# Pooled attention and mixture of depths: the gate taken from the router's scores instead of the gathered rows, and three gathers moved between two chunks' attention

## The chip, the cores and the metric

The kernel runs on one core of one Trainium2 chip. The metric is the device time of one execution in microseconds (us). The median of three runs before the change is 248.09 us (247.69 to 248.15). The profiled execution is a run of 246.4 us whose span, from its first to its last instruction, is 244.6 us. The engines are called as the profile calls them: PE multiplies matrices (PEld is its weight load), DVE and ACT are the vector and the scalar engine, POOL is GpSimd, SP only issues transfers.

## The reference

Two blocks follow each other: attention over keys and values that are averaged in groups of eight, and a feed-forward layer that only the 128 best-scored rows of each batch go through.

```python
B, H, S, D = q.shape                      # 8, 8, 576, 64
k_p = k.reshape(B, H, S//8, 8, D).mean(axis=3)
v_p = v.reshape(B, H, S//8, 8, D).mean(axis=3)
attn = softmax(q @ k_p^T / sqrt(D))       # 576 x 72 for each head
x = (attn @ v_p), heads side by side      # (8, 576, 512)

scores = x @ w_gate                       # (8, 576)
out = x.copy()
for b in range(B):
    top_idx = the 128 rows with the largest scores[b]
    h  = np.maximum(x[b, top_idx] @ w1, 0.0)     # 512 -> 1024
    ye = h @ w2                                  # 1024 -> 512
    g  = 1.0 / (1.0 + np.exp(-scores[b, top_idx]))
    out[b, top_idx] = x[b, top_idx] + g[:, None] * ye
```

The gate g of a chosen row is a function of its score alone, and the score has been computed once already, for all rows, to choose the 128.

## The kernel before, in words

**Attention.** The 576 rows of a batch are cut into chunks of 128 rows. The loop over u (21 units, 0 to 20) takes two chunks at a time: a batch has two units of two chunks each, and the 64 rows left over from two neighbouring batches share one chunk, which is a unit of its own. For an even batch e from 2 on, with s = 6, 11, 16 for e = 2, 4, 6, the units are s and s+1 (batch e), s+2 (the shared chunk of e and o = e+1) and s+3, s+4 (batch o). In each unit `attend` multiplies exponentials with values for both chunks on PE (L371, into the two buffers of the accumulator pA), `norm` divides by the softmax sums on DVE (L379, L387) and puts the scores of the rows into `scs` (L396), `scores` of the next unit runs on PE (L344), its exponentials on ACT (L355 and L349), and `store_x` writes the finished rows to the output (L416, issued by ACT).

**The scores.** The values carry one column more, the pooled value times w_gate (`share_v` L273 on POOL, `gate_v` L277 on DVE), so that attention itself gives the score of every row.

**Choosing and gathering.** `row_bcast` (L438, PE) spreads a batch's scores over all partitions, `count` (L450 and L454, DVE) counts for each row how many are larger, `one_hot` sums the counts on PE (L462) and makes a one-hot matrix OH on DVE (L463, L465). `gather` multiplies OH with `auxb` on PE (L475): auxb holds for each row its number in two bfloat16 parts, so that the two columns of the product add up to the number of the chosen row (`tok`, L477, DVE). POOL turns it into an index (L479) and issues an indirect transfer (L481) that reads the chosen rows back from the output in DRAM into `xr`. It can start only when the batch's stores have landed.

**The feed-forward layer.** `x_trans` transposes xr on PE (L512), `hidden` (L525) and `finish` (L538) are its two products, in float32. `gate` works out g: DVE multiplies xr (128x512) with w_gate, writes the product into `y` (which is only scratch for it) and keeps the sum of each row (L491); ACT takes the exponential (L493); `gate_end` adds one and inverts on DVE (L497, L498). `finish` computes y = p * g + xr on DVE (L539), and POOL scatters y into the output (L541).

**What sets the order.** Nothing is reordered by a scheduler: each engine executes its instructions in the order in which the program emits them. The order around the change is written by hand with `at(u, slot, job)`: a unit runs its attends, slot -1, the norms, slot 0, the next unit's scores, slot 0.5, the stores, and slots 1 to 4. PSUM tiles named `bank` rotate over four banks, which the scores of the next unit all need. POOL also pools keys and values (L246, L247 and L264 to L266); a value pooled late delays `gate_v`, and that the attention which reads the value's extra column.

Of the kernel before, what the change touches and what calls it, by code (L numbers as in the profile page):

```python
# [7 lines left out]
FT = mybir.dt.float32  # L8
BF = mybir.dt.bfloat16
I32 = mybir.dt.int32  # L10
AF = mybir.ActivationFunctionType
OP = mybir.AluOpType
AX = mybir.AxisListType
# [35 lines left out]
def direct_path(ctx, tc, q, k, v, moe_w_gate, moe_w1, moe_w2, moe_capacity, out, flag):  # L49
# [22 lines left out]
    nc = tc.nc  # L72
# [9 lines left out]
    NC = 5  # L82
    C = 128
    HG = H // 2
    R = 2 * TG // POOLW
    DM = H * D
# [4 lines left out]
    cap = int(moe_capacity)  # L91
# [5 lines left out]
    const = ctx.enter_context(tc.tile_pool(name="const", bufs=1))  # L97
# [85 lines left out]
    ones = const.tile([C, 1], BF)  # L183
    one32 = const.tile([C, 1], FT)
    rzall = const.tile([C, NCH, H], FT)
    auxb = [const.tile([C, NC, 2], BF, name=f"auxb{i}") for i in range(2)]
    w1 = const.tile([128, DB, F], FT)
    w2 = const.tile([128, FB, DM], FT)

# [42 lines left out]
    def bank(shape, i=None):  # L232

        if i is None:
            i = turn[0]
        turn[0] = (i + 1) % 4
        return psum.tile(shape, FT, name=f"bank{i}", bufs=1)
# [202 lines left out]

    def count(b):

        CN[b] = work.tile([C, NC], FT, name="cns")
        GE[b] = [work.tile([C, c + 1, C], BF, name=f"ge{c}", bufs=1) for c in range(NC)]
        k = cn[b % 2]
        for c in range(NC):
            s = scs[b % 2][:, c : c + 1]
            n = min(c + 1, NC - 1)
            if c == NC - 1:
                nc.vector.tensor_scalar(GE[b][c][:, 0:n, :], SR[b][0], s, None, op0=OP.is_ge, op1=OP.add,  # L450
                                        accum_out=k[:, c, 1:2])
            x, y, m = ((GE[b][c], SR[b][0][:, 0:n, :], before[:, NC - 1 - n :, :]) if c < NC - 1 else
                       (GE[b][c][:, c : c + 1, :], SR[b][1], before[:, NC - 2 : NC - 1, :]))
            nc.vector.scalar_tensor_tensor(x, y, s, m, op0=OP.is_ge, op1=OP.mult, accum_out=k[:, c, 0:1])  # L454
        nc.vector.tensor_reduce(out=CN[b], in_=k, axis=AX.X, op=OP.add)

    def one_hot(b):

# [11 lines left out]

    def gather(b):

        p = bank([cap, 2], 0 if b == 0 else None)
        for c in range(NC):
            nc.tensor.matmul(p, OH[b][:, c, :], auxb[b % 2][:, c, :], start=(c == 0), stop=(c == NC - 1))  # L475
        tok = work.tile([cap, 1], FT, name="tok")
        nc.vector.tensor_reduce(out=tok, in_=p, axis=AX.X, op=OP.add)  # L477
        idx = work.tile([cap, 1], I32, name="idx")
        nc.gpsimd.tensor_scalar(idx, tok, float(S - 1), float(b * S), op0=OP.min, op1=OP.add)  # L479
        XR[b] = work.tile([cap, DM], FT, name="xr", bufs=3)  # L480
        i = nc.gpsimd.indirect_dma_start(  # L481
            out=XR[b], out_offset=None, in_=out_rows[0 : (b + 1) * S], in_offset=bass.IndirectOffsetOnAxis(ap=idx[:, :1], axis=0))
        others(i, b, (store, scat))
        gath[b] = [i]
        GV[b] = (idx, work.tile([cap, 1], FT, name="g"))

    def gate(b):

        idx, g = GV[b]
        Y[b] = work.tile([cap, DM], FT, name="y")  # L490
        nc.vector.scalar_tensor_tensor(Y[b], XR[b], 1.0, wg[:cap].rearrange("p h d -> p (h d)"), op0=OP.mult, op1=OP.mult,  # L491
                                       accum_out=g)
        nc.scalar.activation(g, g, AF.Exp, scale=-1.0)  # L493

    def gate_end(b):
        idx, g = GV[b]
        nc.vector.tensor_scalar(g, g, 1.0, None, op0=OP.add)  # L497
        nc.vector.reciprocal(g, g)  # L498
# [30 lines left out]
    def finish(b, part, parts, p):  # L529

        idx, g = GV[b]
        if part == 0 and b > 1:
            gate_end(b)
        c = slice(DM // parts * part, DM // parts * (part + 1))
        p = p.rearrange("p a b -> p (a b)")[:cap, 0 : DM // parts]
        for f in range(FB):
            n, m = divmod(f, FB // 2)
            nc.tensor.matmul(p, HT[b, n][:, m, :], w2[:, f, c], start=(f == 0), stop=(f == FB - 1))  # L538
        nc.vector.scalar_tensor_tensor(Y[b][:, c], p, g, XR[b][:, c], op0=OP.mult, op1=OP.add)  # L539
        if part == parts - 1:  # L540
            i = nc.gpsimd.indirect_dma_start(  # L541
                out=out_rows, out_offset=bass.IndirectOffsetOnAxis(ap=idx[:, :1], axis=0), in_=Y[b], in_offset=None)
            others(i, b, (store, scat, gath))
            scat[b] = [i]
# [34 lines left out]
    def at(u, slot, *job):  # L579
        jobs.setdefault((u, slot), []).append(job)  # L580


    pool = nc.gpsimd
    at(2, 2, row_bcast, 0)
    at(2, 2, count, 0)
    at(3, -1, one_hot, 0)
    at(3, -1, gather, 0)
# [7 lines left out]
    at(4, 1, dense, hidden, 0, 0, True)  # L595
    at(4, 1, dense, hidden, 0, 1)
    at(4, 1, k_trans, 2)
    at(4, 1, gate, 0)
    at(4, 1, gate_end, 0)
    at(5, 0, gate_v, 2, 0)  # L600
    at(5, 0, gate_v, 2, 1)
    at(5, 1, row_bcast, 1)
    at(5, 1, count, 1)
    at(5, 1, dense, finish, 0, 0, True, 2)
    at(5, 2, one_hot, 1)
    at(6, -1, gather, 1)
    at(6, 1, dense, finish, 0, 1, True, 2)
    at(7, 0.5, x_trans, 1)
    at(7, 0.5, gate, 1)
    at(8, 1, gate_end, 1)  # L610
    at(7, 2, dense, hidden, 1, 0, True)
    at(8, 2, dense, hidden, 1, 1)
# [2 lines left out]
    for e in range(2, B, 2):  # L615
        s = 6 + 5 * (e // 2 - 1)
        o, last = e + 1, e + 2 == B
        for f in (row_bcast, count):
            at(s + 2, 1, f, e)
            at(s + 4, 0 if last else 1, f, o)  # L620
        at(s + 2, 3, one_hot, e)
        at(s + 3, 3, gather, e)
        if last:
            at(s + 4, 3, x_trans, e)
            at(s + 4, 4, gate, e)
            for f, *x in ((dense, hidden, e, 0), (one_hot, o), (dense, hidden, e, 1), (gather, o), (set_flag,),
                          (dense, finish, e, 0, False, 2), (x_trans, o), (dense, finish, e, 1, False, 2), (gate, o),
                          (dense, hidden, o, 0), (dense, hidden, o, 1), (dense, finish, o, 0)):
                at(s + 5, 1, f, *x)
        else:  # L630
            at(s + 4, 3, one_hot, o)
            at(s + 4, 4, x_trans, e)
            at(s + 4, 4, gate, e)
            at(s + 5, 3, gather, o)
            at(s + 6, 3, x_trans, o)
            at(s + 6, 3, gate, o)
            at(s + 5, 1, dense, hidden, e, 0, True)
            at(s + 5, 2, dense, hidden, e, 1)
            at(s + 6, 1, dense, finish, e, 0, True)
# [15 lines left out]
            at(s + 2, 1, load_v, y)  # L655
            at(s + 2, 2, load_q, y)
            at(s + 2, 4, pool_k, x, pool)
            at(s + 2, 4, pool_v, x, 0, pool, False)
            at(s + 3, 4, share_v, x, 0, pool)
            at(s + 3, 4, pool_v, x, 1, pool)  # L660
            at(s + 3, 0.5, k_trans, x)
            at(s + 4, 1, gate_v, x, 0)
# [25 lines left out]
    def run(u, slot):  # L688
        for f, *x in jobs.pop((u, slot), ()):
            f(*x)  # L690
# [23 lines left out]
    for u in range(NU + 1):  # L714
        mine = [a for a, x in enumerate(chunks) if x[0] == u]
        for a in mine:
            attend(a)
        run(u, -1)
        for a in mine:
            norm(a)  # L720
        run(u, 0)
        if u + 1 < NU:
            scores(u + 1)
        run(u, 0.5)
        if u < NU:
            store_x(u)
        if u + 2 < NU:
            q_trans(u + 2)
        for slot in range(1, 5):
            run(u, slot)  # L730
# [357 lines left out]
```

## Time and profile before

| | |
|---|---|
| device time, median of three | 248.09 us |
| span of the profiled execution | 244.6 us |
| PE busy | 224.1 us (92%) |
| DVE busy | 142.1 us (58%) |
| POOL busy | 130.6 us (53%) |
| ACT busy | 63.6 us (26%) |
| `y<-xr,wg` L491 on DVE | 8 times, 0.68 us median, 3.69 us the longest |
| `tok<-bank` L477 on DVE | 8 times, 0.16 us median |
| `xr<-out_dram,idx`, from issue to landing | 3.4 us the shortest, 4.2 median, 8.4 the longest |

PE is busy nearly all the time, and its idle time is the difference between 244.6 and 224.1 us: 20.5 us, of which 6.7 lie in the first 40 us and 7.6 in the last 15. In the view by windows a row gives the stretch, its length, and for each engine the busy time and the number of instructions; length less PE's busy time is PE's idle time there. In the timeline a row is a start time, a duration, engine, line, operation, and in brackets the time that the engine stood idle before it with what ended the wait. Times on the timeline are counted from the start of the span.

### The profile page before, as it was taken

The page shows a single profiled execution, that of the slowest core. Times are in us where ns is not written, and L with a number is a line of the kernel's source. Part 1 is how long each engine was busy: PE and PEld are TensorE (multiplying, and loading weights), DVE is VectorE, ACT ScalarE, POOL GpSimd, SP SyncE. Part 2 cuts the span into 40 slices and gives each one's busy share as a digit, 9 for nine tenths or more (in the row PEclk, how much of TensorE's full clock was granted, in tenths as well). Part 3 has the DMA queues.
Part 4 walks back from the last instruction along what each step waited for, and adds up shares of the span by engine and source line. Part 5 has one row for each costly group of instructions (what it writes and reads, how often), then busy time and mean ns, then how long its engine had stood idle before and what let it go on. Part 6 is the DMA issues. An engine that isn't in the chain of part 4 may idle for free.

```text
span 244.6 us, 7008 instructions
## 1 busy us (share of the span) xinstructions
PE 224.1 (92%) x2928; PEld 185.0 (76%) x2930; DVE 142.1 (58%) x423; ACT 63.6 (26%) x183; POOL 130.6 (53%) x127
## 2 busy tenths in 40 slices
PE   8989868999999999799989999979989999989980
PEld 4658647899879988699658994769568999979830
DVE  5989776738757878861538957782347337212010
ACT  8233403213311432231113323041114300111100
POOL 8659917995595559596929356594720020121001
PEclk9999999999999999999999999999999999999998
DMA  7999998699716999999509342120411131110001
GB/s 262 349 397 348 381 379 312 204 362 307 256 68 161 366 373 373 383 373 372 187 0 324 155 129 88 44 87 3 131 44 46 47 119 55 43 46 28 19 7 48
DMA packets 14400, 46.94 MB, mean 192 GB/s; under 512 B 1432, under 2 KB 3480, under 8 KB 12312
## 3 DMA queue, kind: packets, MB, share of 16 engines
q1 hardware_dynamic: 9880, 32.77, 37.8%
q10 hardware_dynamic: 3200, 9.44, 11.4%
q0 software_dynamic: 1280, 4.20, 5.2%
q8 instruction: 25, 0.41, 0.7%
q14 instruction: 15, 0.12, 0.2%
HBM read 34.87 MB, written 11.53 MB: 190 GB/s over the span
## 4 chain that ended last, share of the span: by engine, by line
PE 47%; DMA 23%; POOL 13%; DVE 6%; issue 6%; SPq 1%; POOLq 0%; ACT 0%; ACTq 0%
PE bank L538 10%; PE bank L525 9%; PE bank L344 7%; PE pA L371 7%; PE pA L525 6%; PE pA L538 6%; DMA qraw<-in_q_dram 5%; DMA vraw<-in_v_dram 5%; DMA xr<-out_dram,idx 5%; POOL vraw L264 4%; DMA w<-in_moe_w_dram 4%; DMA out_dram<-xs 3%; POOL vraw L265 2%; POOL vp L266 1%; DMA out_dram<-y,idx 1%
## 5 line engine op out<-in xcount | busy, mean ns | idle before, releaser
L355 ACT ACTIVATE et<-bank 128x256 f32<-128x256 f32 x128 | 37.1, 411 | 62.8 <-PE bank L344 62.8
L344 PE MATMUL bank<-qt,kt 32*128 32x256 f32 (+1 forms) x768 | 40.7, 349 | 0.3 <-DVE tok L477 0.3
L525 PE MATMUL bank<-xg,w 128*128 128x128 f32 x320 | 37.6, 276 | 0.2
L371 PE MATMUL pA<-vp,et 128*64 128x66 f32 x1024 | 34.5, 224 | 3.3 <-DVE vp L277 2.3
L525 PEld LDWEIGHTS bank<-xg,w 128*128 128x128 f32 x320 | 36.6, 192 | 1.0 <-ACT et L355 0.9
L371 PEld LDWEIGHTS pA<-vp,et 128*64 128x64 f32 x1024 | 32.1, 137 | 5.7 <-ACT et L355 2.9
L344 PEld LDWEIGHTS bank<-qt,kt 32*128 32x128 f32 x768 | 32.6, 185 | 2.9 <-DVE tok L477 0.3
L264 POOL TENSOR_TENSOR vraw<-vraw 128x1024 f32<-128x1024 f32 x14 | 33.1, 2362 | 2.8 <-DMA vraw<-in_v_dram 2.7
L541 POOL DMA_INDIRECT out_dram<-y,idx x8 | 9.0, 1120 | 45.5 <-DVE y L539 38.3
L538 PE MATMUL bank<-w,ht 128*128 128x256 f32 (+1 forms) x112 | 32.6, 444 | 0.2
L538 PEld LDWEIGHTS bank<-w,ht 128*128 128x128 f32 x112 | 20.7, 190 | 9.3 <-issue 6.7
L538 PE MATMUL pA<-w,ht 128*128 128x256 f32 (+1 forms) x80 | 25.3, 469 | 0.0
L525 PE MATMUL pA<-xg,w 128*128 128x128 f32 x192 | 23.3, 278 | 1.7 <-DVE rzall L379 1.6
L525 PEld LDWEIGHTS pA<-xg,w 128*128 128x128 f32 x192 | 22.0, 192 | 3.5 <-issue 3.0
L329 DVE STREAM_TRANSPOSE qt<-qraw 128x1024 f32<-128x1024 f32 (+1 forms) x24 | 23.0, 967 | 1.5 <-DMA qraw<-in_q_dram 1.5
L479 POOL TENSOR_SCALAR idx<-tok 128x1 int32<-128x1 f32 x8 | 1.8, 223 | 40.0 <-DVE tok L477 36.5
L387 DVE TENSOR_TENSOR xs<-pA,rzall 128x512 f32<-128x512 f32 x32 | 22.1, 691 | 1.1
L538 PEld LDWEIGHTS pA<-w,ht 128*128 128x128 f32 x80 | 14.8, 190 | 8.6 <-issue 7.0
L246 POOL TENSOR_TENSOR kraw<-kraw 128x1152 f32<-128x1152 f32 x7 | 18.5, 2637 | 4.8 <-DVE ge L454 4.7
L539 DVE SCALAR_TENSOR_TENSOR y<-bank,g,xr 128x256 f32<-128x256 f32 (+1 forms) x7 | 3.9, 559 | 26.4 <-PE bank L538 26.4
L265 POOL TENSOR_TENSOR vraw<-vraw 128x512 f32<-128x512 f32 x14 | 17.8, 1271 | 1.1
L454 DVE SCALAR_TENSOR_TENSOR ge<-pA,sc,before 128x128 bf16<-128x128 f32 (+3 forms) x35 | 16.2, 507 | 1.3 <-PE pA L438 1.2
(105 smaller groups left out, 241.6 us busy)
## 6 DMA issues: line engine op xcount, KB each, us to landing
kraw<-in_k_dram SPq DMA_DIRECT2D x8, 1152.0 KB, 9.6
qraw<-in_q_dram SPq DMA_DIRECT2D x8, 1152.0 KB, 13.5
out_dram<-xs ACTq DMA_DIRECT2D x32, 256.0 KB, 3.0
vraw<-in_v_dram SPq DMA_DIRECT2D x7, 1024.0 KB
w<-in_moe_w_dram SPq DMA_DIRECT2D x1, 2048.0 KB
w<-in_moe_w_dram SPq DMA_DIRECT2D x2, 1024.0 KB, 8.6
vraw<-in_v_dram SPq DMA_DIRECT2D x2, 512.0 KB, 7.0
out_dram<-xh ACTq DMA_DIRECT2D x8, 128.0 KB, 6.2
```

The costliest lines, as they stand in the source:

```text
L246: eng.tensor_tensor(out=x[:, :, 0:2, :], in0=x[:, :, 0:2, :], in1=x[:, :, 2:4, :], op=OP.add)
L264: eng.tensor_tensor(out=x[:, :, 0:4, :], in0=x[:, :, 0:4, :], in1=x[:, :, 4:8, :], op=OP.add)
L265: eng.tensor_tensor(out=x[:, :, 0:2, :], in0=x[:, :, 0:2, :], in1=x[:, :, 2:4, :], op=OP.add)
L329: nc.vector.transpose(out=QT[u][:, :, n : n + x.shape[1], :].rearrange("p j t c -> p t j c"), in_=x)
L344: nc.tensor.matmul(p[i][:, s, n, :], KT[x][r, j, s, :], QT[u][r, j, t, G * s : G * s + G], start=(j == 0), stop=(j == 1))
L355: nc.scalar.activation(ET[u][c][i].rearrange("p s (n g t) -> p (s n) g t", n=2, g=G), p[i].rearrange("p s one (n t c g) -> p (s one n) c g ...
L371: nc.tensor.matmul(PA[a][TL * t : TL * t + TL, g, E * n : E * n + E], e, VP[b][:, h, :], start=True, stop=True)
L387: nc.vector.tensor_tensor(out=y[r, i, :].rearrange("p (g n d) -> p g n d", g=2, d=D), in0=o[:, :, :, 0:D], in1=rz.rearrange("p g (n one) - ...
L454: nc.vector.scalar_tensor_tensor(x, y, s, m, op0=OP.is_ge, op1=OP.mult, accum_out=k[:, c, 0:1])
L525: nc.tensor.matmul(p[:, n, :], w1[:, d, 128 * f : 128 * f + 128], XG[b][:, d, :], start=(d == 0), stop=(d == DB - 1))
L538: nc.tensor.matmul(p, HT[b, n][:, m, :], w2[:, f, c], start=(f == 0), stop=(f == FB - 1))
L541: i = nc.gpsimd.indirect_dma_start(out=out_rows, out_offset=bass.IndirectOffsetOnAxis(ap=idx[:, :1], axis=0), in_=Y[b], in_offset=None)
```

## The change

The gate is no longer computed from the gathered rows. A new function `pieces` splits the float32 score of each row into three bfloat16 pieces on POOL: the rounded score, the rounded rest, and the rest of that. They lie beside the two parts of the row number in auxb, so the same five products of `gather` carry them along, with five columns instead of two. One more reduction on DVE adds the three columns of a chosen row to its score. The product of xr and w_gate on DVE goes away, and with it the need to have the gathered row before the gate. `y` is now allocated in `finish`.

Some jobs move. For the even batches 2, 4 and 6 the gather goes from the end of unit s+3 to a new slot -2, between the attends of that unit's two chunks. In the same units the pooling of the next even batch's first half of values is emitted behind the gather, in slot -1 (before: its adds at the end of unit s+2, ahead of the gather, and its product with w_gate behind the gather). The exponential of the gate is emitted soon after its gather. At the end of the program the one-hot and the gather of batch 7 each go ahead of one half of the hidden product of batch 6.

```diff
-    auxb = [const.tile([C, NC, 2], BF, name=f"auxb{i}") for i in range(2)]
+    auxb = [const.tile([C, NC, 5], BF, name=f"auxb{i}") for i in range(2)]
...
-        CN[b] = work.tile([C, NC], FT, name="cns")
+        CN[b] = work.tile([C, NC], FT, name="cns", bufs=1)
...
+    def pieces(b):
+        s, a = scs[b % 2], auxb[b % 2]
+        rest = work.tile([C, NC], FT, name="rest", bufs=1)
+        nc.gpsimd.tensor_copy(a[:, :, 2], s)
+        nc.gpsimd.tensor_tensor(out=rest, in0=s, in1=a[:, :, 2], op=OP.subtract)
+        nc.gpsimd.tensor_copy(a[:, :, 3], rest)
+        nc.gpsimd.tensor_tensor(out=a[:, :, 4], in0=rest, in1=a[:, :, 3], op=OP.subtract)
...
     def gather(b):
-        p = bank([cap, 2], 0 if b == 0 else None)
+        p = bank([cap, 5], 0 if b == 0 else None)
...
-        nc.vector.tensor_reduce(out=tok, in_=p, axis=AX.X, op=OP.add)
+        nc.vector.tensor_reduce(out=tok, in_=p[:, 0:2], axis=AX.X, op=OP.add)
...
-        GV[b] = (idx, work.tile([cap, 1], FT, name="g"))
+        g = work.tile([cap, 1], FT, name="g")
+        GV[b] = (idx, g)
+        nc.vector.tensor_reduce(out=g, in_=p[:, 2:5], axis=AX.X, op=OP.add)
     def gate(b):
         idx, g = GV[b]
-        Y[b] = work.tile([cap, DM], FT, name="y")
-        nc.vector.scalar_tensor_tensor(Y[b], XR[b], 1.0, wg[:cap].rearrange("p h d -> p (h d)"), op0=OP.mult, op1=OP.mult,
-                                       accum_out=g)
         nc.scalar.activation(g, g, AF.Exp, scale=-1.0)
...
     def finish(b, part, parts, p):
-        if part == 0 and b > 1:
-            gate_end(b)
+        if part == 0:
+            Y[b] = work.tile([cap, DM], FT, name="y")
+            if b > 1:
+                gate_end(b)
...
+    at(2, 2, pieces, 0)
...
-    at(4, 1, gate, 0)
+    at(3, 1, gate, 0)
...
+    at(5, 1, pieces, 1)
...
-    at(7, 0.5, gate, 1)
+    at(6, 1, gate, 1)
...
+        at(s + 2, 1, pieces, e)
+        at(s + 4, 0 if last else 1, pieces, o)
         at(s + 2, 3, one_hot, e)
-        at(s + 3, 3, gather, e)
+        at(s + 3, -2, gather, e)
+        at(s + 3, 3, gate, e)
         if last:
             at(s + 4, 3, x_trans, e)
-            at(s + 4, 4, gate, e)
-            for f, *x in ((dense, hidden, e, 0), (one_hot, o), (dense, hidden, e, 1), (gather, o), (set_flag,),
-                          (dense, finish, e, 0, False, 2), (x_trans, o), (dense, finish, e, 1, False, 2), (gate, o),
+            for f, *x in ((one_hot, o), (dense, hidden, e, 0), (gather, o), (dense, hidden, e, 1), (gate, o), (set_flag,),
+                          (dense, finish, e, 0, False, 2), (x_trans, o), (dense, finish, e, 1, False, 2),
                           (dense, hidden, o, 0), (dense, hidden, o, 1), (dense, finish, o, 0)):
...
-            at(s + 4, 4, gate, e)
             at(s + 5, 3, gather, o)
             at(s + 6, 3, x_trans, o)
-            at(s + 6, 3, gate, o)
+            at(s + 5, 4, gate, o)
...
-            at(s + 2, 4, pool_v, x, 0, pool, False)
-            at(s + 3, 4, share_v, x, 0, pool)
+            at(s + 3, -1, pool_v, x, 0, pool)
             at(s + 3, 4, pool_v, x, 1, pool)
...
         for a in mine:
             attend(a)
+            if a == mine[0]:
+                run(u, -2)
         run(u, -1)
```

## The prediction

> **What bounds the kernel now.** I read the page's busy times first, then the windows, then who waited for whom, and last the timeline around each wait of PE. PE is busy for 224.1 of 244.6 us, so the time is PE's work plus PE's idle time. The windows say where the idle time lies:
>
> ```profile
> 88.00:104.00 16.00, 14.66 (x203) 12.35 (x199) 12.21 (x35) 5.33 (x18) 12.19 (x11) 1.00 1.02 387
> 104.00:120.00 16.00, 16.00 (x273) 14.65 (x269) 8.35 (x26) 4.72 (x14) 13.77 (x11) 1.00 0.89 325
> 120.00:140.00 20.00, 19.34 (x240) 14.68 (x240) 12.04 (x38) 4.50 (x14) 11.46 (x9) 1.00 0.51 171
> 140.00:160.00 20.00, 19.31 (x261) 13.95 (x259) 13.70 (x34) 5.07 (x17) 11.22 (x10) 1.00 0.26 80
> 160.00:180.00 20.00, 19.00 (x221) 14.82 (x223) 8.49 (x27) 4.77 (x15) 12.53 (x11) 1.00 0.23 67
> 180.00:200.00 20.00, 19.34 (x319) 17.77 (x320) 11.84 (x45) 6.62 (x20) 2.52 (x3) 1.00 0.18 56
> 215.00:230.00 15.00, 14.01 (x98) 12.88 (x97) 1.95 (x7) 1.41 (x4) 2.27 (x2) 1.00 0.11 37
> ```
>
> Length less PE's busy time, the second and third numbers, is 1.34, 0, 0.66, 0.69, 1.00, 0.66 and 0.99 us: 5.3 us of idle time between 88 and 230 us, in small pieces. The clock (1.00) is full everywhere. The DMA share next to last says that transfers fill the engines until about 120 us and have room afterwards. PE's waits in the timeline are these:
>
> ```profile
> 102.49 0.63 PE L512 MATMUL bank<-ident,xr 128*128 128x128 f32 x4 [1.25 <-DMA xr<-out_dram,idx]
> ...
> 127.34 0.68 PE L371 MATMUL pA<-vp,el 128*64 128x66 f32 x14 [0.62 <-DVE vp L277]
> ...
> 161.00 2.25 PE L525 MATMUL pA<-xg,w 128*128 128x128 f32 x18 [1.59 <-DVE rzall L379]
> ...
> 181.30 0.68 PE L371 MATMUL pA<-vp,el 128*64 128x66 f32 x14 [0.62 <-DVE vp L277]
> ...
> 219.26 0.63 PE L512 MATMUL bank<-ident,xr 128*128 128x128 f32 x4 [0.99 <-DMA xr<-out_dram,idx]
> ```
>
> Two wait for gathered rows, two for `vp` L277, one for the norm on DVE. What DVE did just before the last three is the gate's product:
>
> ```profile
> 126.26 0.68 DVE L491 SCALAR_TENSOR_TENSOR y<-xr,wg 128x512 f32<-128x512 f32 x1
> 126.87 0.08 DVE L491 DVE_READ_ACCUMULATOR y<-xr,wg 128x1 f32 x1
> 126.87 0.42 DVE L277 TENSOR_REDUCE vp<-vraw 128x4 f32<-128x256 f32 x1
> ...
> 156.23 3.69 DVE L491 SCALAR_TENSOR_TENSOR y<-xr,wg 128x512 f32<-128x512 f32 x1
> 159.85 0.08 DVE L491 DVE_READ_ACCUMULATOR y<-xr,wg 128x1 f32 x1
> 159.85 0.20 DVE L379 RECIPROCAL rzall<-pA 128x8 f32<-128x8 f32 x1
> ```
>
> At 126 us (and alike at 180) L491 stands in front of L277. At 156 us it takes 3.69 us instead of 0.68, while POOL adds keys (L246, 156.73 to 159.36), and the norm that frees pA for PE comes after it.
>
> **What the Trainium skill says.** "SBUF — State Buffer", section "Who interferes with whom": a DVE instruction with two SBUF inputs contends with a GpSimd instruction that reads SBUF, and the loser waits for the whole instruction. L491 has two (xr, wg); the 3.69 us, ending just after POOL's add, agree. "DMA: Bandwidth & Descriptors", section "Issuing engines are not separate DMA queues": transfers of all engines share the same 16 DMA engines. The gather at 93.91 us landed after 8.44 us at DMA share 1.02, the last one after 3.44 us at 0.11, which agrees. "TensorE: Matmul & The Clock Gate", section "The mechanism": matmuls start and end strictly in order. So a gather that waits between two chunks holds back the second chunk and all behind it.
>
> **The change, part by part.** Removed: eight L491 (0.68 + 0.08 us each). Added on DVE: eight reductions of 128x3; the nearest row is L477 (128x2, 0.16 us median). That is 8 x 0.6 = 4.8 us less DVE work, worth something only where PE waits behind it:
>
> - At 126 and 180 us, L277 starts when L539 ends (126.26) and is done 0.42 us later, at 126.68. PE has finished its first 18 products at 126.72, so both waits go: 2 x 0.62 = 1.24.
> - At 156 us the norm follows L465 (ends 156.23) and the first chunk's products (about 156.4). L379, L387 and L396 take about 1.2 us, so pA is free near 157.7, before PE ends its scores (159.4). The whole 1.59 goes. No other DVE instruction there has two SBUF inputs.
>
> Moved, the even gather. Batch 2's is at 92.15 us on PE, its index comes on POOL behind the pooling at 93.33, and its rows land at 102.35. Between the attends of unit 9 (84.63 to 86.65) its products fall at about 85.9, `tok` at 86.3, the index at 86.6. POOL can then issue the transfer if the batch's last store has landed: it was issued until 81.45, and stores of `xh` took 5.9 to 6.4 us, so near 87.2. POOL's own pooling could not begin before 88.73 anyway (`vraw` landed then), so the gather lies in POOL's wait. With the same 8.4 us the rows land near 96, and x_trans needs them at 101.2: 1.25 gone. Behind the gather POOL's chain from L264 to the second L273 takes 88.73 to 100.94 less the 1.7 us of index and gather, and ends near 99.3; its `vp` is ready before the attends at 101.9.
>
> The price of the new place: OH must be ready in mid-attend. At unit 9 L465 runs 85.00 to 85.82, while the first chunk's half of 2.02 us ends at 85.64. L475 started 0.06 us after L465 in the first batch, so PE stands still for 0.24 us. Units 14 (135.82 against 136.01 + 0.06) and 19 (189.78 against 189.95 + 0.06) give 0.25 and 0.23: together 0.7. The bounds are 0, if the first half ends later than at the middle of the row, and 0.4 each, if the way to DVE and back costs more: 0 to 1.2. DVE then does both reductions before its norm, 0.65 us later; its idle gaps behind (1.49, 1.66 and 4.79 us in the three units) take that.
>
> Added, five columns instead of two: five products are 0.10 us on the chain with 2 columns, and I take no difference. A batch's bank is now released one reduction later. For batches 0 and 1 the next scores need that bank at once (L344 waited 0.25 us for `tok` at 37.06, and took 2.33 instead of 2.01 us at 61.52): 0.15 each, 0.3 together. For the others a whole chunk or other products lie between: nothing.
>
> Added on POOL, `pieces`: four instructions of 128x5. Nearest rows are L211 (128x4, 0.27 us) and L212 (128x1, 0.18 us), so about 1 us a batch. The first waits for the last score of the batch. In five batches POOL is idle then (it waits 3 to 15 us for `tok` in the rows of L479), for batches 3 and 5 it sits behind pooling that the scores precede. Batch 4 differs: at 127.87 L246 would now start after the score at 129.3 and the pieces, 2.4 us later. Behind it are L247, then the gather (POOL had 6.5 us idle before it at 143.0) and then values, which I find done near 149, before the 150.9 of now. So nothing.
>
> The tail: one-hot and gather of batch 7 each go one half of hidden (3.6 us) earlier. From gather to landing it is now 214.23 to 219.12, 4.9 us. Moved to 210.5 it lands near 215.4, and the transposes follow at 217.8: 0.99 gone. The other gate exponentials and the `bufs=1` only move on ACT and DVE, which are in order and have gaps.
>
> Sum: removed 1.25 + 1.24 + 1.59 + 0.99 = 5.07; added 0.7 + 0.3 = 1.0. Net 4.05, and 248.09 - 4.05 = 244.0 us.
>
> **Rivals.**
>
> 1. *A store wait replaces the gather wait.* If the last store of batch 2 lands late (the longest `xs` store took 8.8 us, which gives 89.7), POOL waits at the gather with all value pooling queued behind it, DVE's L277 waits for POOL and PE's attends for L277. At 89.7 the pooling chain still just fits (90.9 + 10.5 = 101.4, and L277 at 101.8). Each further us is lost, and at 1.25 the first saving is gone: 245.3. With twice the price for the mid-attend gathers, 246. For it: DMA is full there. Against it: the `xh` stores show 5.9 to 6.4.
> 2. *Nothing is paid.* The stalls in mid-attend fall into gaps, all idle time goes, and the loads that wait behind L491 at 74.82 (through a memset on DVE) start 1.4 us earlier and help: 248.09 - 5.3 = 242.8. Against it: there is hardly a gap left on PE to take a stall.
> 3. *Slower.* TensorE's order makes each even gather a real wait: if DVE or POOL is 1.2 us later than I think in each of three units (3.6), and POOL's block at the stores delays the values of unit 11 by 2.3 us more, the sum is 3.6 + 2.3 - 5.07 + 0.3 = +1.1: 249.2. Against it: DVE's order puts one-hot directly before the gather, and nothing but PE's own L462 releases it.
> 4. *No change*: rival 3 at about two thirds. 248.
>
> **How the numbers follow.** Forecast as worked out: 0.67. Rival 1: 0.15. Rival 2: 0.07. Rival 4: 0.03. Rival 3: 0.08. Faster 0.89, same 0.03, slower 0.08. The low end takes the stalls at zero: 244.0 - 1.1 = 242.9. The high end takes in rival 1 with dearer stalls: 246.2. Rivals 3 and 4 and the edge of 2 stay outside.
>
> **What would show it.** In the profile after: no L491; PE's waits for `xr` gone at about 101 and 217; no wait for L277 at the shared chunks; PE going from L344 to L525 without a gap near 158; new waits of PE on L465 of about 0.25 us in three units. Wrong it is if POOL's gather of batch 2 is seen waiting on `out_dram<-xs` or `xh` beyond 89.7 us, if PE waits for `vp` in unit 11, or if the new waits on L465 are 1 us and more.

## The result, and the profile after

The changed kernel takes 244.67 us (median of four runs, 243.99 to 245.74), the kernel before beside it 248.0 us (247.69 to 248.15): ratio 0.9871, 95% interval 0.9834 to 0.9909. Two later series gave 0.9839 (0.9789 to 0.9889) and 0.9822 (0.976 to 0.9883). The forecast was 244.0 us. Ratios, here and below, leave out slow runs, which took over 1.5% longer than the fastest of the same kernel; medians do not.

The same stretches in the view by windows, of the kernel after:

```profile
88.00:104.00 16.00, 15.90 (x226) 13.43 (x228) 12.59 (x38) 5.30 (x18) 12.02 (x14) 1.00 0.98 375
104.00:120.00 16.00, 16.00 (x262) 14.75 (x259) 8.58 (x28) 4.81 (x15) 14.31 (x11) 1.00 0.85 293
120.00:140.00 20.00, 19.87 (x243) 14.82 (x242) 11.29 (x37) 4.27 (x13) 10.78 (x13) 1.00 0.56 184
140.00:160.00 20.00, 19.90 (x262) 14.52 (x261) 12.65 (x42) 5.37 (x18) 13.17 (x15) 1.00 0.21 69
160.00:180.00 20.00, 19.99 (x247) 15.64 (x246) 7.01 (x19) 5.17 (x16) 12.90 (x12) 1.00 0.22 68
180.00:200.00 20.00, 19.87 (x303) 18.04 (x298) 10.62 (x42) 5.92 (x19) 3.48 (x11) 1.00 0.23 72
215.00:230.00 15.00, 15.00 (x99) 13.24 (x98) 1.19 (x4) 1.78 (x3) 1.02 (x1) 1.00 0.06 20
```

Length less PE's busy time adds up to 0.47 us, from 5.34. PE's waits over the whole program (us in total, times, longest) all lie ahead of 80 us now: no row names `xr` any more, and none has `hidden` waiting for `rzall`.

```profile
PE pA L371 <- DVE vp L277: 2.4, 3, 1.4
PE pA L371 <- ACT et L355: 1.2, 2, 0.7
PE pA L125 <- DVE zeros L119: 1.2, 1, 1.2
PE pA L519 <- DVE xg L522: 1.0, 2, 0.5
PE bank L438 <- ACT et L355: 0.8, 1, 0.8
PE bank L471 <- DVE ge L450: 0.5, 1, 0.5
PE bank L344 <- DVE rzall L379: 0.4, 1, 0.4
PE pA L371 <- ACT el L349: 0.3, 1, 0.3
```

PE's timeline at three of the five places (x_trans is L519 now, hidden L532): no bracket, so no wait.

```profile
102.20 0.64 PE L519 MATMUL bank<-ident,xr 128*128 128x128 f32 x4
...
157.69 2.01 PE L344 MATMUL bank<-qt,kt 32*128 32x256 f32 x32
159.63 3.84 PE L532 MATMUL pA<-xg,w 128*128 128x128 f32 x32
...
216.95 0.60 PE L519 MATMUL bank<-ident,xr 128*128 128x128 f32 x4
```

DVE's timeline around 126 and 156 us: L277 follows `finish` (L548) directly, and the norm L379 stands 0.75 us after the one-hot matrix (L474), waiting for nothing but its products.

```profile
126.00 0.75 DVE L548 SCALAR_TENSOR_TENSOR y<-pA,g,xr 128x512 f32<-128x512 f32 x1 [5.99 <-PE pA L547]
126.67 0.41 DVE L277 TENSOR_REDUCE vp<-vraw 128x4 f32<-128x256 f32 x1
...
155.71 0.82 DVE L474 TENSOR_TENSOR oh<-slots,bank 128x640 bf16<-128x640 f32 x1
157.28 0.21 DVE L379 RECIPROCAL rzall<-pA 128x8 f32<-128x8 f32 x1 [0.75 <-PE pA L371]
```

What is new: PE's weight load waits for OH in mid-attend, in units 9, 14 and 19,

```profile
86.55 0.19 PEld L484 LDWEIGHTS <-oh 128*128 128x128 bf16 x5 [0.23 <-DVE oh L474]
...
135.85 0.19 PEld L484 LDWEIGHTS <-oh 128*128 128x128 bf16 x5 [0.23 <-DVE oh L474]
...
188.34 0.19 PEld L484 LDWEIGHTS <-oh 128*128 128x128 bf16 x5 [0.22 <-DVE oh L474]
```

and POOL stands at the gather of batch 2 until the last store lands, 3.4 us later than I had put it. Its pooling of values ends behind that, at 102.34 us (101.66 and 0.68), not at 99.3:

```profile
87.33 0.23 POOL L488 TENSOR_SCALAR idx<-tok 128x1 int32<-128x1 f32 x1
90.73 1.08 POOL L490 DMA_INDIRECT xr<-out_dram,idx  x1 [3.17 <-DMA out_dram<-xh]
91.83 2.36 POOL L264 TENSOR_TENSOR vraw<-vraw 128x1024 f32<-128x1024 f32 x1
...
101.66 0.68 POOL L273 TENSOR_TENSOR vraw<-vp,wg 128x256 f32<-128x256 f32 x1
```

### The profile page after: what moved, and what is told of

Same layout as the page of the kernel before. It is cut to its first block, busy times and chain, and to the rows that moved or that the text cites. A ratio compares the mean times of both kernels' runs of the same rounds, so it can differ in the third digit from the quotient of the medians.

```text
span 242.2 us, 7047 instructions
## 1 busy us (share of the span) xinstructions
PE 226.3 (93%) x2930; PEld 186.1 (77%) x2930; DVE 134.0 (55%) x415; ACT 63.0 (26%) x183; POOL 135.2 (56%) x159
## 4 chain that ended last, share of the span: by engine, by line
PE 79%; POOL 8%; DVE 8%; issue 2%; ACT 1%; POOLq 0%; DVEq 0%; ACTq 0%
PE bank L532 15%; PE bank L344 14%; PE bank L547 13%; PE pA L371 12%; PE pA L547 10%; PE pA L532 9%; POOL vraw L264 2%; DVE oh L474 1%; PE bank L471 1%; PE bank L519 1%; PE pA L438 1%; POOL kraw L246 1%; POOL vraw L265 1%; DVE vraw L264 1%; POOL vraw L273 1%
## 5 line engine op out<-in xcount | busy, mean ns | idle before, releaser
L344 PE MATMUL bank<-qt,kt 32*128 32x256 f32 (+1 forms) x768 | 41.9, 350 | 0.4 <-DVE rzall L379 0.4
L371 PE MATMUL pA<-vp,et 128*64 128x66 f32 x1024 | 35.3, 224 | 3.5 <-DVE vp L277 2.4
L532 PE MATMUL bank<-xg,w 128*128 128x128 f32 x320 | 37.6, 276 | 0.2
L532 PEld LDWEIGHTS bank<-xg,w 128*128 128x128 f32 x320 | 36.5, 192 | 1.0 <-ACT et L355 0.9
L344 PEld LDWEIGHTS bank<-qt,kt 32*128 32x128 f32 x768 | 33.6, 185 | 3.2 <-issue 0.6
L550 POOL DMA_INDIRECT out_dram<-y,idx x8 | 8.4, 1045 | 46.3 <-DVE y L548 23.0
L532 PE MATMUL pA<-xg,w 128*128 128x128 f32 x192 | 23.4, 278 | 0.1
L532 PEld LDWEIGHTS pA<-xg,w 128*128 128x128 f32 x192 | 22.0, 192 | 1.9 <-issue 1.0
L379 DVE RECIPROCAL rzall<-pA 128x8 f32<-128x8 f32 (+1 forms) x37 | 7.5, 204 | 25.2 <-PE pA L371 25.1
L548 DVE SCALAR_TENSOR_TENSOR y<-bank,g,xr 128x256 f32<-128x256 f32 (+1 forms) x7 | 3.9, 559 | 26.2 <-PE bank L547 26.2
L454 DVE SCALAR_TENSOR_TENSOR ge<-pA,sc,before 128x128 bf16<-128x128 f32 (+3 forms) x35 | 16.2, 508 | 0.9 <-PE pA L438 0.7
```

The costliest lines, as they stand in the source:

```text
L344: nc.tensor.matmul(p[i][:, s, n, :], KT[x][r, j, s, :], QT[u][r, j, t, G * s : G * s + G], start=(j == 0), stop=(j == 1))
L371: nc.tensor.matmul(PA[a][TL * t : TL * t + TL, g, E * n : E * n + E], e, VP[b][:, h, :], start=True, stop=True)
L532: nc.tensor.matmul(p[:, n, :], w1[:, d, 128 * f : 128 * f + 128], XG[b][:, d, :], start=(d == 0), stop=(d == DB - 1))
L550: i = nc.gpsimd.indirect_dma_start(out=out_rows, out_offset=bass.IndirectOffsetOnAxis(ap=idx[:, :1], axis=0), in_=Y[b], in_offset=None)
```

## The experiments

PE executes in order, so a loss or gain stays in the start times of everything behind it, unless a later wait takes it up. "Scores 12" are the scores that unit 12 uses. The table is worked out from PE's timelines: the start of the scores (L344) of a unit, in each run, less the start in the kernel before (37.06, 77.71, 86.65, 105.07, 127.95, 136.83, 170.44, 181.91 and 190.79 us), and the same for x_trans of batch 7 (219.26) and the end of the span (244.60).

| at | after | again | gate only | moves only | one input | gathers late | one reduction | old gathers | best |
|---|---|---|---|---|---|---|---|---|---|
| scores 4 | +0.18 | +0.17 | +0.29 | +0.37 | +0.01 | +0.33 | +0.05 | +0.16 | +0.11 |
| scores 9 | +0.68 | +0.30 | +1.05 | +0.37 | +0.01 | +0.98 | +0.23 | +0.45 | +0.10 |
| scores 10 | +1.20 | +0.82 | +1.05 | +0.89 | +0.01 | +0.98 | +0.75 | +0.45 | +0.10 |
| scores 12 | -0.28 | -0.66 | -0.26 | -0.59 | +0.04 | -0.04 | -0.73 | -0.70 | -1.16 |
| scores 14 | -0.20 | -1.27 | -0.87 | +0.78 | +0.03 | -0.65 | -1.34 | -1.31 | -1.77 |
| scores 15 | +0.32 | -0.75 | -0.87 | +1.30 | +0.03 | -0.65 | -0.82 | -1.31 | -1.77 |
| scores 18 | -1.34 | -2.48 | -2.49 | +1.20 | -1.59 | -2.25 | -2.55 | -2.92 | -3.39 |
| scores 19 | -1.67 | -3.08 | -3.10 | +1.20 | -1.60 | -2.86 | -3.16 | -3.53 | -4.00 |
| scores 20 | -1.16 | -2.57 | -3.10 | +1.72 | -1.60 | -2.86 | -2.65 | -3.53 | -4.00 |
| x_trans 7 | -2.31 | -3.72 | -3.18 | +0.57 | -1.64 | -3.89 | -3.80 | -4.58 | -5.05 |
| end | -2.40 | -3.76 | -3.23 | +0.53 | -1.35 | -4.19 | -4.14 | -4.65 | -5.41 |

My theory is the sum of the prediction: five waits go, three gathers cost a stall each. The rivals are that gate or moves alone do it all, that L491's 3.69 us have another cause than POOL, and that the moved gathers are what brings batch 2's rows in time.

### The changed kernel again

> The changed kernel once more, beside the others of this set. Theory: 244.0 to 245.0 us against 248.0 before. It is also the second trace in which to look for the three places where the scores' products took 0.25 to 0.45 us longer than their row before (near 105, 117 and 169 us): if they come back at the same places, something in the program causes them; if not, they are chance.

Measured: 243.51 us (242.45 to 245.11), ratio 0.9839 (0.9789 to 0.9889). The steps of the table return to 0.01 us where the program sets them: +0.52 at scores 10, 15 and 20, -1.63 between scores 17 and 18, -0.6 before scores 14 and 19 (where longer scores hide 0.25 and 0.28 us of it in the first profile). What does not return: 0.25 us at the start of unit 4, and three scores of 2.45, 2.26 and 2.29 us instead of 2.01 (at 104.79, 116.64 and 169.10 us of the first profile) at full granted clock. They make up most of the 1.36 us between the two ends. I found no cause for them. Two of the three do return later: at scores 13 and 18 the third profile of this program ("side by side", below) has 2.25 and 2.29 us, and the other three profiles of that series have 2.23 to 2.28 us there, the kernel before with one job moved among them. The eight profiles of the two series between have 2.01 or 2.02 us. So these two are not tied to the change, and I count none of them as a step of it.

### The gate from the scores alone

The changed kernel with its moves taken back:

```diff
-        at(s + 3, -2, gather, e)
-        at(s + 3, 3, gate, e)
+        at(s + 3, 3, gather, e)
+        at(s + 3, 4, gate, e)
...
-            for f, *x in ((one_hot, o), (dense, hidden, e, 0), (gather, o), (dense, hidden, e, 1), (gate, o), (set_flag,),
+            for f, *x in ((dense, hidden, e, 0), (one_hot, o), (dense, hidden, e, 1), (gather, o), (gate, o), (set_flag,),
...
-            at(s + 3, -1, pool_v, x, 0, pool)
+            at(s + 2, 4, pool_v, x, 0, pool, False)
+            at(s + 3, 4, share_v, x, 0, pool)
```

> The new gate alone: pieces, five columns and the second reduction stay, the product of xr and w_gate stays away, but the even gathers, the pooling of values behind them and the order at the end are those of before. Theory: the two waits for L277 at the shared chunks (1.24 us) and the wait of 1.59 us near 160 us go; the waits for gathered rows (1.25 and 0.99 us) stay; the second reduction costs 0.3 to 0.6 us on batches 0 and 1. So 248.0 - 2.83 + 0.4 = 245.6 us. Rival (the gain comes from the moved gathers): 247.7 us or more.

Measured: 243.08 us (242.62 to 246.14), ratio 0.9845 (0.9784 to 0.9907): level with the whole change. My expectation was 2.5 us too high, in part because the kernel before was itself faster in this series (247.33 us, not 248.0); by the spans it gained 3.23 us where I had put 2.43. Its PE timeline has the tail's wait, but none for batch 2:

```profile
102.22 0.63 PE L519 MATMUL bank<-ident,xr 128*128 128x128 f32 x4
...
216.08 0.63 PE L519 MATMUL bank<-ident,xr 128*128 128x128 f32 x4 [0.91 <-DMA xr<-out_dram,idx]
```

So the gate alone removes the waits at 126, 160 and 180 us, and the first one too, with the gather in its old place. In this run PE was also 1.05 us late by scores 9; the run called best in the table, which is not late there, shows the same without that, but a second profile of that kernel, below, waits 0.55 us for these rows.

### The moves alone

The kernel before with the moves:

```diff
-        at(s + 3, 3, gather, e)
+        at(s + 3, -2, gather, e)
...
-            for f, *x in ((dense, hidden, e, 0), (one_hot, o), (dense, hidden, e, 1), (gather, o), (set_flag,),
+            for f, *x in ((one_hot, o), (dense, hidden, e, 0), (gather, o), (dense, hidden, e, 1), (set_flag,),
...
-            at(s + 2, 4, pool_v, x, 0, pool, False)
-            at(s + 3, 4, share_v, x, 0, pool)
+            at(s + 3, -1, pool_v, x, 0, pool)
...
             attend(a)
+            if a == mine[0]:
+                run(u, -2)
```

> The moves alone: the even gathers between two chunks' attends and the end's order are the new ones, the gate is still the product of xr and w_gate (L491) at its old places. Theory: the waits of PE for gathered rows go (1.25 and 0.99 us), each even gather costs PE 0.4 us (1.2 in all), and the waits behind L491 stay: 248.0 - 2.24 + 1.2 = 247.0 us. Rival (an early gather is worth more, since it also frees POOL): 246 us or less.

Measured: 247.18 us (246.59 to 250.6), ratio 1.0002 (0.9973 to 1.0031): nothing gained, where I had expected 1 us. The wait for batch 2's rows goes and the tail gains 1.05 us (scores 20 plus 0.10 behind it, to x_trans 7), the gathers take 3 x 0.52. And one loss is new, just behind scores 12. DVE, POOL and PE in the timeline there:

```profile
103.06 3.67 DVE L491 SCALAR_TENSOR_TENSOR y<-xr,wg 128x512 f32<-128x512 f32 x1
103.53 2.64 POOL L246 TENSOR_TENSOR kraw<-kraw 128x1152 f32<-128x1152 f32 x1
...
107.81 3.81 PE L525 MATMUL pA<-xg,w 128*128 128x128 f32 x32 [1.33 <-DVE rzall L379]
```

With the rows in time, the product L491 of batch 2, 0.68 us in the kernel before, now meets POOL's addition of keys, as that of batch 4 did, and PE waits 1.33 us for the norm behind it. So the moves make the collision, and the gate takes it away.

### The product with one input

```diff
-        nc.vector.scalar_tensor_tensor(Y[b], XR[b], 1.0, wg[:cap].rearrange("p h d -> p (h d)"), op0=OP.mult, op1=OP.mult,
-                                       accum_out=g)
+        nc.vector.tensor_scalar(Y[b], XR[b], 0.0, None, op0=OP.mult, op1=OP.add, accum_out=g)
```

The kernel before, with an instruction of the same size in the place of L491. It reads no w_gate, so the gate is a constant.

> The kernel before with one edit: L491 reads xr alone (multiplied by zero, with its sum kept) in place of xr and w_gate, over the same 128x512. The gate is therefore a constant and the chosen rows are not the reference's. Theory (two SBUF inputs wait for POOL's instruction): the longest L491 falls from 3.69 us to about 0.7 us, PE's wait of 1.59 us near 160 us goes, the two waits of 0.62 us behind L491 stay; 248.0 - 1.6 = 246.4 us. Rival (L491 was long for another reason, such as its wait for the rows or its length): it stays near 3.7 us and the time near 248.

Measured: 245.65 us (244.44 to 249.58), ratio 0.9938 (0.991 to 0.9967). DVE, POOL and PE at the place where L491 took 3.69 us:

```profile
156.27 0.68 DVE L491 TENSOR_SCALAR_CACHE_REDUCE y<-xr 128x512 f32<-128x512 f32 x1
156.76 2.63 POOL L246 TENSOR_TENSOR kraw<-kraw 128x1152 f32<-128x1152 f32 x1
...
156.87 0.20 DVE L379 RECIPROCAL rzall<-pA 128x8 f32<-128x8 f32 x1
...
159.38 3.84 PE L524 MATMUL pA<-xg,w 128*128 128x128 f32 x32
```

POOL's addition is at the same place and as long as before; the DVE instruction has its 0.68 us, the wait of 1.59 us is gone, and nothing else in the table moves by more than 0.04 us up to scores 20. This is what the Trainium skill says ("SBUF — State Buffer", section "Who interferes with whom"): a DVE instruction with two SBUF inputs contends with a GpSimd instruction that reads SBUF, and one with at most one, outside the 2-port modes that the page names, doesn't. The kernel before, the moves alone and this run show both sides.

The edit changed the operation too, not only the number of inputs. But L454 in the kernel before has the operation of L491, with an accumulator as well, and reads one matrix from PSUM (`pA`) and one from SBUF (`before`). It takes 0.75 us beside POOL's addition and 0.75 us where POOL is idle, so the operation alone is not the cause:

```profile
98.11 1.28 POOL L265 TENSOR_TENSOR vraw<-vraw 128x512 f32<-128x512 f32 x1
98.33 0.75 DVE L454 SCALAR_TENSOR_TENSOR ge<-pA,sc,before 128x512 bf16<-128x512 f32 x1
...
185.87 0.75 DVE L454 SCALAR_TENSOR_TENSOR ge<-pA,sc,before 128x512 bf16<-128x512 f32 x1
```

### The even gathers behind the next scores

The changed kernel with one more move:

```diff
-        at(s + 3, -2, gather, e)
+        at(s + 3, 0.5, gather, e, True)
...
-            at(s + 3, -1, pool_v, x, 0, pool)
+            at(s + 3, 0.5, pool_v, x, 0, pool)
```

With True the product goes into a buffer of pA instead of a bank.

> The changed kernel, but the even gathers stand behind the next unit's scores, in an accumulator, and no longer between the attends. Theory (PE's strict order: each mid-attend gather costs about 0.5 us, of which 0.23 is the wait for the one-hot matrix and the rest the small products and the refill): the start of scores 10, 15 and 20 stops moving by +0.52 each, the rows of batch 2 still land in time because the gather on POOL waits for the store until about 90.6 us in any case, and the kernel gains 1.0 to 1.5 us on the changed one: about 4.5 to 5.0 us under the kernel before, ratio near 0.981. Rival (the products cost the same wherever they stand, or the later index delays POOL's values): within 0.3 us of the changed kernel, ratio 0.984 to 0.987.

Measured: 242.53 us (241.37 to 243.43), ratio 0.9779 (0.9722 to 0.9836). Its PE timeline, unit 9:

```profile
85.61 2.09 PE L371 MATMUL pA<-vp,et 128*64 128x66 f32 x64
87.63 2.01 PE L344 MATMUL bank<-qt,kt 32*128 32x256 f32 x32
89.58 0.28 PE L484 MATMUL pA<-auxb,oh 128*128 128x5 bf16 x5
89.72 3.70 PE L547 MATMUL pA<-w,ht 128*128 128x256 f32 x16
```

The table has no step at scores 10, 15 and 20: the +0.52 belong to the place in mid-attend, not to the products, which take 0.14 us of PE here. The later index costs nothing, for POOL waits for the store anyhow (its gather started at 91.35, against 90.73). The 0.98 us at scores 9 lie ahead of the edit; among them PE waited 0.28 us for w2 at 56.1 us.

### One reduction for row number and score

The changed kernel with a sixth column:

```diff
-    auxb = [const.tile([C, NC, 5], BF, name=f"auxb{i}") for i in range(2)]
+    auxb = [const.tile([C, NC, 6], BF, name=f"auxb{i}") for i in range(2)]
...
-        nc.vector.tensor_reduce(out=tok, in_=p[:, 0:2], axis=AX.X, op=OP.add)
+        nc.vector.tensor_reduce(out=both, in_=p.rearrange("p (k c) -> p k c", k=2), axis=AX.X, op=OP.add)
...
-        nc.vector.tensor_reduce(out=g, in_=p[:, 2:5], axis=AX.X, op=OP.add)
```

Column 2 is zero, and the pieces are columns 3 to 5.

> The changed kernel with six columns (a zero column between), so that one reduction gives both the row number and the score and the bank is free earlier. Theory (the second reduction holds the bank): scores 4 and 7 start 0.1 to 0.15 us earlier each, as in the kernel before, 0.2 to 0.3 us in all: ratio lower than the changed kernel's by about 0.001. Rival (the longer product and the wider reduction cost the same): no difference in the start of scores 4 and 7.

Measured: 242.6 us (242.25 to 244.35), ratio 0.9799 (0.9744 to 0.9853). Scores 4 start 0.12 us earlier than in the second profile of the changed kernel, and the scores of unit 7 take 2.33 us again instead of 2.48. The total is too small to be told by the times alone.

### Old gathers, new tail, without and with one reduction

The gate-only kernel with the changed order of the tail:

```diff
-            for f, *x in ((dense, hidden, e, 0), (one_hot, o), (dense, hidden, e, 1), (gather, o), (gate, o), (set_flag,),
+            for f, *x in ((one_hot, o), (dense, hidden, e, 0), (gather, o), (dense, hidden, e, 1), (gate, o), (set_flag,),
```

and the same with the six columns of the last experiment (its diff again).

> The gate from the scores and the new order of the tail, but the even gathers and the pooling around them in their old places. Theory: as in the run with the gate alone no PE time is lost at scores 10, 15 and 20, and the waits at 126, 160 and 180 us are gone (3.1 us by scores 20); the tail adds 0.9 to 1.1 us: 4.0 to 4.3 us under the kernel before by span, ratio 0.982 to 0.984. Rival (the even gathers in mid-attend are what removed the wait for the rows of batch 2): a wait for those rows of 0.5 to 1.2 us comes back, and it is no faster than the changed kernel.

Measured: 242.81 us (241.82 to 243.92), ratio 0.9803 (0.9749 to 0.9857).

> As the run before it in this list (gate from the scores, even gathers in the old place, new tail), with six columns and one reduction. Theory: both savings add, 4.3 to 4.6 us under the kernel before, ratio about 0.982. Rival: no faster than with two reductions.

Measured: 241.78 us (240.98 to 242.7), ratio 0.9755 (0.9703 to 0.9807), the lowest of all. Its PE timeline (x_trans is L519, the scores are L345, attend L372):

```profile
37.17 2.01 PE L345 MATMUL bank<-qt,kt 32*128 32x256 f32 x32 [0.26 <-DVE both L487]
...
84.73 2.09 PE L372 MATMUL pA<-vp,et 128*64 128x66 f32 x64
86.75 2.01 PE L345 MATMUL bank<-qt,kt 32*128 32x256 f32 x32
...
101.32 0.63 PE L519 MATMUL bank<-ident,xr 128*128 128x128 f32 x4
```

It gained 0.76 us of span on the run without the single reduction. That is more than I expected (4.3 to 4.6 us under the kernel before; it is 5.41). 0.35 us of the 0.76 lie before scores 9, where both places of the second reduction are; the rest, 0.12 us between scores 10 and 12 and 0.29 behind the last x_trans, I can't assign. The attend is whole, and the rows are there although the gather goes out at 94.0 us, no earlier than before (93.91). They land after 7.2 us instead of 8.4. The rival of the old-gather runs, that the wait would return without the move, has fallen for these two profiles; a second profile of the last kernel, below, has part of the wait.

### Why the rows come earlier: the loads

The gate's product stood ahead of a memset on DVE that releases the loads of batch 4. In the kernel before, these started at 74.82 us, in the best run at 73.44. Two runs ask whether that is the cause: the kernel before with the product of batch 1 behind the memset, and the best kernel with two idle passes ahead of it.

```diff
-    at(7, 0.5, gate, 1)
...
     at(NU - 1, 4, check_range)
+    at(7, 0.5, gate, 1)
```

So the gate is emitted last in its slot.

> The kernel before with one job moved: the gate of batch 1 is emitted behind the memset that the loads of batch 4 wait for, so the loads start near 73.4 us instead of 74.8. Theory A (the rows of batch 2 come in time in the gate-alone kernels because the loads have left the DMA engines earlier): the wait of 1.25 us for these rows at 102.5 us shrinks to 0.3 us or less, 247.0 us. Theory B (the start of the loads is not what decides, as the run with one SBUF input says, whose loads started 0.9 us earlier with the wait unchanged): the wait stays within 0.3 us of 1.25, ratio 0.999 to 1.002.

```diff
+    def hold():
+        Y[1] = work.tile([cap, DM], FT, name="y")
+        held = work.tile([cap, 1], FT, name="held", bufs=1)
+        for _ in range(2):
+            nc.vector.tensor_scalar(Y[1], XR[1], 0.0, None, op0=OP.mult, op1=OP.add, accum_out=held)
...
     at(7, 0.5, x_trans, 1)
+    at(7, 0.5, hold)
```

> The run with the old gathers and one reduction, with two DVE passes over 128x512 (0.68 us each, their result is not used) ahead of the same memset, so that the loads of batch 4 start near 74.8 us again as in the kernel before. Theory A (the early loads are what saves the wait for the rows of batch 2): a wait of about 1.2 us for these rows comes back at 102 us, and 1.2 us are lost. Theory B: no wait there, within 0.3 us of the run without the passes.

The first, with its loads at 73.76 us, gave 247.71 us (246.72 to 250.84), ratio 0.9966 (0.9938 to 0.9995), and PE still waits:

```profile
102.86 0.63 PE L512 MATMUL bank<-ident,xr 128*128 128x128 f32 x4 [1.19 <-DMA xr<-out_dram,idx]
```

The second, with its loads at 75.06 us, gave 242.63 us (242.21 to 244.65), ratio 0.9766 (0.969 to 0.9842), with a wait that is neither 0 nor 1.2 us:

```profile
102.47 0.63 PE L525 MATMUL bank<-ident,xr 128*128 128x128 f32 x4 [0.82 <-DMA xr<-out_dram,idx]
```

And the best kernel, run once more below, has a wait of 0.55 us there itself, with its loads at 73.47 us. So the start of the loads of batch 4 alone doesn't decide: the first run refutes it, the second says no more than that 0.3 us may hang on it.

What divides the traces is another wait, that of the next load of keys (batch 5) on SP's queue. Its row in the kernel before:

```profile
SPq L111 <- DMA kraw<-in_k_dram: 3.9, 1, 3.9
```

and in the kernel after, where the load behind it has taken over that wait:

```profile
SPq L138 <- DMA kraw<-in_k_dram: 5.2, 1, 5.2
```

The instructions of the built programs say why. The transfers that SP and ACT issue share eight completion counters, and a load waits until the counter it uses is free. By these waits, batch 5's keys use counter 2 in every kernel that I compared; batch 4's keys use counter 2 in the four kernels with the old gate (before, moves only, one input, loads first), and counter 3 (4 with the idle passes) in those with the new one. So in the four the load of 1152 KB goes out at 79.9 to 82.0 us, when batch 4's keys have landed, and in the others at 76.4 to 78.3. With the gather in its old place the rows take 8.4, 8.5 and 8.4 us in the former and 7.1, 7.3, 7.2, 8.0 and 7.8 in the latter. Where the gather is moved, the store that it waits for landed by 87.7 us with the late load (moves only) and near 90.6 with the early one (after). Both fit a load that leaves the shared DMA engines earlier, ahead of the stores. That the numbering is the cause was not tried by itself.

### The changed kernel and the best one, side by side

> The changed kernel beside the next one, for their direct comparison. 3.3 to 3.8 us under the kernel before, ratio 0.984 to 0.987; in the records, scores 10, 15 and 20 late by 0.52 us each.

Measured: 245.18 us (243.78 to 247.53), ratio 0.9822 (0.976 to 0.9883). The three steps of 0.5 us are there again. Its profiled run lost 1.65 us more in the scores of unit 4 (3.66 instead of 2.01 us, granted clock 0.7 of full speed in that slice of the page), and the longer scores 13 and 18 of the first profile stand in it again, as told above.

> The version with the old gathers, the new tail and one reduction, once more on the same chip as the changed kernel. Span 5.0 to 5.5 us under the kernel before, 1.2 to 1.8 us under the changed kernel, ratio to before 0.976 to 0.980.

Measured: 243.1 us (242.26 to 244.61), ratio 0.9777 (0.9721 to 0.9832). Of its span it gained 4.06 us on the kernel before, about 1 to 1.4 less than expected: it waits for batch 2's rows, which took 7.8 us,

```profile
101.93 0.63 PE L519 MATMUL bank<-ident,xr 128*128 128x128 f32 x4 [0.55 <-DMA xr<-out_dram,idx]
```

and lost 0.25 and 0.27 us in the same longer scores 13 and 18. On one chip, the medians of the runs that enter the two ratios are 243.1 us and, for the changed kernel, 244.9 us: 1.8 us apart; by the ratios it is 0.0045, about 1.1 us. The intervals of the two ratios to the kernel before overlap; that it is faster than the changed kernel rests on this pair, on the earlier one (0.9755 against 0.9799 for the changed kernel with one reduction, in one series), and on the steps in the table. Whether the old place of the even gathers is better than the one behind the scores is not shown: those two runs stand at 0.9803 and 0.9779 in one series, and the place behind the scores was not tried with one reduction.

## Why the prediction was right

The time was right by 0.7 us, and the steps can be read off one by one in the second profile of the changed kernel (column "again"), whose span is 3.76 us shorter than before.

| step | predicted | measured |
|---|---|---|
| wait for batch 2's rows | -1.25 | -1.38 (scores 11 to 12) |
| L277 behind L491, twice | -1.24 | -0.61 and -0.60 |
| accumulator freed late at 160 us | -1.59 | -1.63 |
| rows of batch 7 | -0.99 | -1.05 |
| three gathers in mid-attend | +0.7 | +1.56 where they stand now, -0.30 where they stood |
| bank held longer, batches 0 and 1 | +0.3 | +0.30 |

**The four savings.** All were paid in full, at the sizes of the waits. The mechanism of 160 us, the two SBUF inputs, was argued in the prediction and is shown now: one input alone removes 1.6 us there, and the moves alone make a second collision of the same kind. That pooling of batch 4's keys, the pieces on POOL and the rows from the tail's earlier gather would fit in was right: no wait for any of them shows.

**The gathers: the term that was too small.** I took 0.24 us, the time that PE stands still for OH. That wait is in the trace, 0.23, 0.23 and 0.22 us. But each gather moves the next scores by 0.52 us. The rest, 0.29, is the five products (0.21 from 86.55 us to the second attend at 86.76) and a second attend that takes 1.09 us, to the scores at 87.85, instead of the half of 2.02; against that stand 0.10 us saved where the gather stood. I had left both out, as if moving the products cost nothing because there are as many as before. Net it is 1.26 us instead of 0.7, just above my upper bound of 1.2. The order of matmuls that the Trainium skill gives ("TensorE: Matmul & The Clock Gate", section "The mechanism") explains the part that I priced, the second attend held back by a wait; the 0.29 is a price that only the trace shows.

**The first saving: right in size, with two links wrong.** The store landed near 90.6 us, not 87.2. POOL's gather waiting beyond 89.7 was one of my own signs of being wrong, and it is there: rival 1 was nearer than its chance of 0.15 says. At 89.7 I had the pooling just fit, with each further us lost. It did fit at 90.6: POOL issued the gather at once, its chain ended at 102.34, DVE's L277 waited 0.70 us for it (0.39 in the kernel before) and was done at 102.80, and PE, whose attends began at 102.76 instead of the 101.9 I had put, shows no wait. That the saving came out whole is therefore in part luck. The late store fits a key load that now goes ahead of it, an effect of the change that I had not looked for: with the moves alone, where that load goes out at 82.0 us as before, the store landed by 87.7, close to my figure. And the move was not needed for most of this saving: with the new gate and the gather in its old place, three profiles show no wait for the rows and one 0.55 us (0.82 with the idle passes).

**Rival 2** (nothing is paid, 242.8) fell by the stalls, and nothing of rivals 3 and 4 shows. The idle time in the seven stretches did vanish, 4.87 us of it, but PE's busy time rose by 2.2 us (224.1 to 226.3). I read the rise as loss that is booked as busy: the 0.29 us of each gather, and the longer scores of this profile; in the second profile, without them, PE is busy for 225.1 us.

**From 4.05 to 3.3.** The measured steps add up to 3.71 us, and the second profile's span is 3.76 us shorter. The first series' medians gave 3.3 us and its profile 2.4; the difference of the profiles is mostly the unexplained stretches of 0.25 to 0.44 us, which come and go between profiles of the same program. One sum of the prediction is off by 0.1: its low end takes away 1.1 us of added cost, though the added terms make 1.0.

## What to carry to other kernels

A product that only serves to recompute what the program already knows is worth its whole wait, not its busy time: look for the instruction behind it in its engine's order, and for POOL work beside it if it reads two SBUF tiles. A small product between two streams on a full PE can cost more than the wait that the trace names (here 0.52 us against 0.23); put it where the stream changes anyway, behind the scores here, and take from a combined change only the parts whose steps are negative. The fastest version tried keeps the gate from the scores and the new tail, leaves the even gathers in their old place and sums row number and score in one reduction: 241.78 and 243.1 us in its two series, ratios 0.9755 and 0.9777.

## What the runs showed that I had not expected

The new gate changed which completion counter a load used, and another load started earlier (77.40 us in the gate-only run instead of 81.85), with no line changed that issues a load. A DVE instruction with two SBUF inputs can be held by a POOL addition that starts after it: in the moves-only run L491 is on record from 103.06 us, during POOL's scatter (102.47 to 103.50), before the addition of keys (103.53), and ends only 0.56 us after that (106.17). That the scatter held it first would explain this, but no run shows it. And the rows of batch 2 took 7.2 and 7.8 us in two profiles of one kernel, which alone moves its end by half a microsecond: no single profile settles a wait on a transfer that lands so close.
